# Nineteen small loads behind the third K and V transfer of a decode block on one core

## The chip, the core and the metric

The kernel runs on one core of a Trainium2 chip. The metric is the device time of one execution in microseconds, as the median of several runs. The profile is a single profiled execution on the same core, with the time of every instruction and every DMA packet.

## The reference

A transformer block for one token of each of four sequences (B = 4, D = 512), in float32. The conditioning `c` gives six modulation vectors. Attention has 32 query heads on 8 K/V heads of width 128 and sees the last 2048 positions of the cache; a gated feed-forward network of width 1792 follows.

```python
mod = (_silu(c) @ w_mod).reshape(c.shape[0], 6, 1, -1)
sa, ca, ga, sb, cb, gb = (mod[:, 0], ..., mod[:, 5])
h = _layernorm(x, axis=-1) * (1 + ca) + sa
x = x + ga * _A_ref(h, A_k_cache, A_v_cache, A_wq, A_wo)   # softmax(q k^T / sqrt(128)) v, then @ wo
h = _layernorm(x, axis=-1) * (1 + cb) + sb
x = x + gb * _B_ref(h, B_w1, B_w3, B_w2)                   # (silu(h @ w1) * (h @ w3)) @ w2
```

## The kernel before

About 101 MB are read once, and almost every tile is a slice of one SBUF ring of 192 KB for each partition, cut into three slots of 64 KB. Seven K/V groups of 8 MB each come in one transfer (`kv_in`, K in the first half of a row, V in the second); the eighth is split into `last_k_wo` and `last_v`, and the weights `wo`, `w1`, `w3` and `w2` follow. All but `wq` (ScalarE's queue) are issued by SyncE, in the order of the program text, and one transfer has 128 rows.

A helper `do` (line 57, to which the profile puts every operation) records each operation with the regions that it reads and writes. From these it derives the waits: an operation waits for the last one on another engine that touched an overlapping region, and for each DMA that did, unless it is known to be done already. Every awaited DMA has a semaphore of its own. Waits of one operation are put out in falling order of the position that the awaited operation has on its engine. Loads wait for whoever last read their slot, and this sets the order of the transfers:

- The first three loads on SP are `w_mod_a` (slot 0) and K/V group 0 (slot 2), at once, and group 1 (slot 0) when TensorE has done the modulation products.
- Group 2 goes to slot 1 when `wq` has been used. This is the "third K and V transfer", `kv[2]`.
- Group g + 3 is issued when group g has been finished, into the same slot; the first of these is `kv[3]`, behind group 0.
- Behind group 4 come the weights for the projection and the second modulation (`wom`), behind group 6 the last K and V, `wo` and `w1`; `w3` waits for the second modulation's products (`mod_columns` into `mod_b`), and `w2` comes in four pieces behind it.

The work of a group is scores on TensorE, the maximum on VectorE, the exponential on ScalarE, transposes, and the products with V. In the last part `mod_b` (128 x 512) takes the second modulation: four quarters `ga`, `sh`, `cb1` and `gb`. `x1` (128 x 128) is the residual after attention, and `h2T` (128 x 4 x 32) the transposed input of the feed-forward part, written by `transposed("h2T")`. The gate products read `h2T` and `w1`, the next ones `h2T` and `w3`, and `w2` follows.

Near the end a mark splits the program in two parts. The semaphores of the first part are cleared by GpSimd in one range when the other engines have passed the mark.

Of the kernel before, what the change touches and what calls it, by code (L numbers as in the profile page):

```python
# [9 lines left out]
P = 128  # L10
# [135 lines left out]
def block_kernel(nc, w_mod_a, wq, kv_in, wo_mod, last_k_wo, last_v, wo, w1, w3, w2, out):  # L146
# [5 lines left out]
    do = Program(nc)  # L152

    def sb(name, *shape):
        return nc.alloc_sbuf_tensor(name, (P, *shape), F32).ap()
# [12 lines left out]
    def bank():  # L168
        turn[0] += 1
        return banks[turn[0] % 2]  # L170

    def load(dst, src, cuts=(0, 1), queue="sync"):
        step = src.shape[1] // cuts[-1]
        for lo, hi in zip(cuts[:-1], cuts[1:]):
            do(queue, "dma_start", dst[:, lo * step : hi * step], src[:, lo * step : hi * step])
        return dst[:, : src.shape[1]]
# [59 lines left out]
    xc, sq, h = (sb(n, P) for n in ("xc", "sq", "h"))  # L236
# [20 lines left out]
    def transposed(name):  # L257
        hp = bank()[:, :P]
        do("tensor", "transpose", hp, h, ident)
        hT = sb(name, 4, 32)  # L260
        do("vector", "tensor_copy", hT.rearrange("p j i -> p (j i)"), hp)
        return hT

# [20 lines left out]
    do("vector", "tensor_scalar_add", mod_a[:, P:], mod_a[:, P:], 1.0)  # L284
    modulate(mod_a[:, P:], mod_a[:, :P])
    hT = transposed("hT")
    kv[1] = load(slots[0], kv_in[1])


    work = sb("work", 512)  # L290
    for half in range(2):
        qp = s_ps[half]
        for k in range(4):
            for i in range(4):
                at = ((half * 4 + i) * 4 + k) * 512
                do("tensor", "matmul", qp[32 * i : 32 * i + 32, :], hT[:, k, :], wq_t[:, at : at + 512], start=(k == 0), stop=(k == 3))
    for half in range(2):
# [4 lines left out]
        for i in range(R):  # L302
# [5 lines left out]
                src[:, :, :, None].to_broadcast([P, 4, B, NC]),  # L308
            )
    kv[2] = load(slots[1], kv_in[2])  # L310

    def project_out(g):
        for i in range(R):
            do("tensor", "matmul", a_ps[32 * i : 32 * i + B, :], oT[:, g, i, :], wo_t[g][:, i, :], start=(g == 0), stop=(g == G - 1))
# [70 lines left out]
        project_out(g)  # L385
    heads_out(G - 2)

    mod_b = sb("mod_b", 512)
    ga, sh, cb1, gb = (mod_b[:, i * P : (i + 1) * P] for i in range(4))
    mod_columns(wom[:, HALF:].rearrange("p (k j i) -> p k j i", k=4, j=4), mod_b, 4)  # L390
    do("vector", "tensor_scalar_add", cb1, cb1, 1.0)
# [8 lines left out]
    attn = bank()  # L400
    for j in range(4):
        do("tensor", "matmul", attn[32 * j : 32 * j + 32, :P], spread, work[:, j * P : (j + 1) * P], start=True, stop=True)
    x1, ag, tot2 = sb("x1", P), sq, sb("tot2", 1)
    do("vector", "tensor_mul", ag, attn[:, :P], ga)
    do("vector", "scalar_tensor_tensor", x1, ag, 1.0, x_sb, op0=ALU.mult, op1=ALU.add, accum_out=tot2)
    norm(x1, tot2)
    modulate(cb1, sh)
    h2T = transposed("h2T")

    H = P // 2  # L410
# [40 lines left out]
    for n in range(W2_CUTS[1]):  # L451
        i = n % 4
# [62 lines left out]
```

## Time and profile before

| what | value |
|---|---|
| median of two runs | 242.44 us (242.40 to 242.47) |
| the profiled execution, first to last instruction | 241.1 us |
| TensorE busy / VectorE busy / ScalarE busy | 146.8 / 55.2 / 24.0 us |
| bytes moved, mean rate | 101.38 MB, 421 GB/s |
| DMA packets in all / of SP's queue | 2889 / 2736 |
| packets under 512 bytes | 448 |
| mean granted TensorE clock | 0.865 |

The profile doesn't give what lies outside the first and the last instruction; the runs' median is 1.3 us above the span. In rows of the time line the first number is the start, the second the length, both in us; x7 after a row is the number of instructions merged in it, and a bracket gives the idle time of the engine before it and what ended it. "SPq" is SyncE's queue with its issues, whose length is that of the issuing instruction and not of the transfer. In the DMA lists the last number is the time from issue to landing.

### The profile page before, as it was taken

Reading aid. Unit: us, or ns where it says so; the run is one execution under the profiler, and the core shown is the slowest. Engines: PE = TensorE matmul, PEld = TensorE weight load, DVE = VectorE, ACT = ScalarE, POOL = GpSimd, SP = SyncE. Lnnn points to the kernel's source line nnn. Section 1 sums busy time; section 2 is a strip of 40 time slices with the busy share of each in tenths; the row PEclk is TensorE's granted clock in tenths of the full one; section 3 lists DMA queues with packets and bytes.
Section 4 is the critical chain, followed back from the end, with each engine's and each line's share of the span. In section 5 each row is a group of like instructions: output and inputs, shape, how many; then the busy total and the mean of one; then the engine's idle time right before and its main releaser. Section 6 shows DMA issues by size and latency. Waiting matters only on the chain.

```text
span 241.1 us, 2468 instructions
## 1 busy us (share of the span) xinstructions
PE 146.8 (61%) x1103; PEld 52.8 (22%) x1103; DVE 55.2 (23%) x140; ACT 24.0 (10%) x36; POOL 2.6 (1%) x11
## 2 busy tenths in 40 slices
PE   0000169756782972945767586567296919964876
PEld 0000132213222312201311222221131202422333
DVE  4000220240303124123132124130312014103120
ACT  2000000103003003001200300300300000320100
POOL 3000000000000000000000000000000000000000
PEclk9999997995977799779797589797977997996899
DMA  8999989898989898989999999999999999999993
GB/s 316 414 436 425 500 370 500 351 511 359 511 359 503 370 502 370 489 383 478 391 479 391 478 394 468 402 468 405 457 413 424 435 405 435 407 432 426 416 415 133
DMA packets 2889, 101.38 MB, mean 421 GB/s; under 512 B 448, under 2 KB 448, under 8 KB 704
## 3 DMA queue, kind: packets, MB, share of 16 engines
q1 hardware_dynamic: 2736, 92.85, 89.5%
q10 hardware_dynamic: 144, 8.39, 8.1%
q8 instruction: 8, 0.13, 0.2%
q14 instruction: 1, 0.01, 0.0%
HBM read 101.20 MB, written 0.03 MB: 420 GB/s over the span
## 4 chain that ended last, share of the span: by engine, by line
DMA 73%; PE 20%; DVE 3%; ACT 2%; issue 0%; SPq 0%
DMA ring<-kv_in 30%; DMA ring<-wo_mod 17%; DMA ring<-w 15%; DMA ring<-w_mod_a 11%; PE s_ps L57 8%; PE bank L57 7%; PE o_ps L57 4%; PE a_ps L57 2%; ACT p_sb L57 2%; DVE nm L57 2%; DVE p_sb L57 0%; DVE e L57 0%; DVE sq L57 0%; DVE xc L57 0%; DVE tot L57 0%
## 5 line engine op out<-in xcount | busy, mean ns | idle before, releaser
L57 PE MATMUL s_ps<-ring,qT 128*32 128x512 f32 x256 | 37.0, 731 | 20.2 <-DMA ring<-kv_in 14.7
L57 PE MATMUL bank<-ident,p_sb 128*128 128x128 f32 (+1 forms) x136 | 27.4, 350 | 30.8 <-ACT p_sb L57 30.7
L57 PE MATMUL o_ps<-ring,pT 128*16 128x512 f32 x256 | 37.8, 696 | 0.0
L57 PEld LDWEIGHTS bank<-ident,p_sb 128*128 128x128 f32 (+1 forms) x136 | 19.6, 177 | 51.9 <-ACT p_sb L57 31.7
L57 ACT ACTIVATE p_sb<-s_ps,nm 128x2048 f32<-128x2048 f32 (+1 forms) x11 | 16.5, 1501 | 143.2 <-DVE oT L57 105.2
L57 DVE TENSOR_REDUCE nm<-s_ps 128x1 f32<-128x2048 f32 x7 | 16.0, 2292 | 34.5 <-PE s_ps L57 34.5
L57 DVE COPY pT<-bank 128x64 f32<-128x64 f32 x32 | 7.2, 224 | 56.1 <-PE bank L57 56.1
L57 PEld LDWEIGHTS s_ps<-ring,qT 128*32 128x32 f32 x256 | 9.0, 131 | 47.5 <-issue 20.7
L57 PE MATMUL bank<-ident,xs 128*128 128x128 f32 x1 | 0.5, 473 | 27.8 <-POOL xs L57 27.8
L57 PE MATMUL s_ps<-ring,h2T 128*32 128x512 f32 (+1 forms) x64 | 9.1, 664 | 2.3 <-DMA ring<-w 2.3
L57 PE MATMUL a_ps<-ring,oT 128*4 128x512 f32 x64 | 9.1, 709 | 2.0 <-DMA ring<-wo_mod 2.0
L57 PE MATMUL s_ps<-ring,hT 128*32 128x512 f32 x64 | 8.8, 711 | 0.4 <-DVE hT L57 0.4
L57 PEld LDWEIGHTS o_ps<-ring,pT 128*16 128x16 f32 x256 | 5.4, 98 | 11.6 <-issue 9.2
L57 DVE SCALAR_TENSOR_TENSOR o_own<-o_ps,rl,own 128x512 f32<-128x512 f32 x7 | 5.3, 751 | 11.1 <-PE o_ps L57 11.1
L57 DVE TENSOR_REDUCE o_sum<-o_own 128x128 f32<-128x512 f32 x7 | 7.2, 1029 | 0.2
L57 PE MATMUL bank<-ring,sc 128*32 128x256 f32 (+1 forms) x64 | 7.2, 610 | 0.0
L57 PEld LDWEIGHTS bank<-ident,xs 128*128 128x128 f32 x1 | 0.2, 180 | 27.8 <-POOL xs L57 27.8
L57 DVE TENSOR_SCALAR e<-e 128x16 f32<-128x16 f32 x1 | 0.2, 174 | 23.8 <-ACT e L57 23.8
L57 DVE TENSOR_REDUCE mx<-s_ps 128x1 f32<-128x512 f32 x4 | 2.8, 691 | 7.6 <-PE s_ps L57 7.6
L57 DVE COPY qT<-bank 128x64 f32<-128x64 f32 x8 | 2.2, 277 | 9.8 <-PE bank L57 9.4
L57 PEld LDWEIGHTS s_ps<-ring,h2T 128*32 128x32 f32 x64 | 2.6, 129 | 7.4 <-issue 4.5
L57 PE MATMUL s_ps<-ring,hidT 128*32 128x64 f32 (+1 forms) x126 | 3.7, 262 | 0.3 <-DVE hidT L57 0.3
(93 smaller groups left out, 55.4 us busy)
## 6 DMA issues: line engine op xcount, KB each, us to landing
ring<-w SPq DMA_DIRECT2D x2, 3584.0 KB, 38.3
ring<-last_k_wo SPq DMA_DIRECT2D x1, 6144.0 KB, 30.5
ring<-last_v SPq DMA_DIRECT2D x1, 4096.0 KB, 39.9
ring<-w_mod_a SPq DMA_DIRECT2D x1, 2064.0 KB, 26.6
ring<-wo SPq DMA_DIRECT2D x1, 2048.0 KB, 43.4
ring<-w SPq DMA_DIRECT2D x1, 1792.0 KB, 40.9
ring<-w SPq DMA_DIRECT2D x1, 1024.0 KB, 42.9
ring<-w SPq DMA_DIRECT2D x1, 512.0 KB, 43.7
```

Source lines behind the costliest of these rows:

```text
L57: op = Op(engine, lambda: getattr(getattr(self.nc, engine), method)(*args, **kw), [])
```

## The change

Nineteen loads are added on SP, behind the issue of `kv[2]` and ahead of that of `kv[3]`. Fifteen of them read n rows of 4n columns (16n bytes) of `w1`, for n = 1 to 15, into the first n partitions of `mod_b`, each into columns of its own. Four read 64, 32, 8 and 112 rows of 68, 76, 80 and 72 columns into parts of `x1` and `h2T`. All of what they write is overwritten later by the copy into `mod_b`, the sum into `x1` and the copy into `h2T`. These three tiles are allocated earlier for it. The helper derives new waits: the copy into `mod_b` waits for fifteen loads, the sum for three, and the copy into `h2T` for one.

```diff
@@ transposed @@
-        hT = sb(name, 4, 32)
+        hT = h2T if name == "h2T" else sb(name, 4, 32)
@@ behind kv[2] @@
     kv[2] = load(slots[1], kv_in[2])
+    mod_b = sb("mod_b", 512)
+    for n in range(1, 16):
+        at = 2 * n * (n - 1)
+        do("sync", "dma_start", mod_b[:n, at : at + 4 * n], w1[:n, at : at + 4 * n])
+    x1, h2T = sb("x1", P), sb("h2T", 4, 32)
+    h2T_rows = h2T.rearrange("p j i -> p (j i)")
+    for dst, rows, n in ((x1[:64, :68], 64, 68), (x1[64:96, :76], 32, 76), (x1[96::4, :80], 8, 80), (h2T_rows[:112, :72], 112, 72)):
+        do("sync", "dma_start", dst, w1[:rows, 1024 : 1024 + n])
@@ ahead of the second modulation @@
-    mod_b = sb("mod_b", 512)
@@ behind the attention @@
-    x1, ag, tot2 = sb("x1", P), sq, sb("tot2", 1)
+    ag, tot2 = sq, sb("tot2", 1)
```

## The prediction

> **What bounds the kernel now.** I read the page first: the span, the row of DMA slices, the queue table and the chain that ended last.
>
> ```profile
> span 241.1 us, 2468 instructions
> ...
> DMA  8999989898989898989999999999999999999993
> ...
> q1 hardware_dynamic: 2736, 92.85, 89.5%
> ...
> DMA 73%; PE 20%; DVE 3%; ACT 2%; issue 0%; SPq 0%
> ```
>
> The DMA engines are at nine tenths or more in nearly every slice, and transfers are 73% of the chain. The 2736 packets of SP's queue are nineteen loads and stores of 144: 128 rows and sixteen more, one for each engine's signal at the end. The second view is the table by stages (length, the engines, the granted TensorE clock, the DMA share, GB/s).
>
> ```profile
> 34.00:67.00 33.00, 22.69 (x157) 7.80 (x153) 9.12 (x23) 3.25 (x4) 0.00 (x0) 0.84 0.99 429
> 67.00:86.00 19.00, 13.93 (x82) 4.93 (x82) 3.81 (x8) 2.06 (x2) 0.00 (x0) 0.73 1.01 435
> 86.00:143.00 57.00, 38.03 (x246) 13.38 (x246) 14.88 (x27) 6.17 (x6) 0.00 (x0) 0.82 1.02 439
> 143.00:183.00 40.00, 25.31 (x172) 8.52 (x164) 11.51 (x20) 4.12 (x4) 0.00 (x0) 0.87 0.97 419
> 183.00:229.00 46.00, 33.46 (x239) 11.13 (x239) 9.32 (x32) 5.32 (x14) 0.00 (x0) 0.85 1.00 428
> ```
>
> The share is 0.97 to 1.02 from 34 to 229 us, at 419 to 439 GB/s, while PE is busy for two thirds of the time at a clock below full. The kernel is a stream of loads that never runs dry; arithmetic follows each landing. So any time that the DMA engines lose before the last weights arrive is lost to the end, and any time that SP, DVE or PE lose beside a full queue is not.
>
> The third view is SP's own time line, with the consumers on PE, around the place of the edit.
>
> ```profile
> 45.73 0.33 SPq L57 DMA_DIRECT2D ring<-kv_in  x1
> ...
> 48.17 3.64 PE L57 MATMUL s_ps<-ring,qT 128*32 128x512 f32 x32 [0.57 <-DMA ring<-kv_in]
> ...
> 64.81 0.33 SPq L57 DMA_DIRECT2D ring<-kv_in  x1
> ...
> 67.28 0.64 PE L57 MATMUL s_ps<-ring,qT 128*32 128x512 f32 x4 [2.54 <-DMA ring<-kv_in]
> ...
> 86.77 0.64 PE L57 MATMUL s_ps<-ring,qT 128*32 128x512 f32 x4 [1.32 <-DMA ring<-kv_in]
> ```
>
> The third K and V transfer is issued at 45.73 and used at 86.77. The fourth is issued at 64.81, when group 0 has freed its slot, and until 86.77 it only stands behind the third. So SP idles for 64.81 - 46.06 = 18.7 us behind the edit, and a late fourth issue would start to hurt only near 86.8, 40 us later.
>
> **The change part by part.** Nothing is removed. Nineteen loads are added to SP's program behind the issue at 45.73, and the copies that later fill `mod_b`, `x1` and `h2T` get waits for them. The moved allocations issue nothing.
>
> *SP.* The price of an issue is in the rows of the weight loads.
>
> ```profile
> L57 SPq DMA_DIRECT2D ring<-w x6: 327/438/453, 181.6 to 194.7; - x6
> ...
> 194.18 0.94 SPq L57 DMA_DIRECT2D ring<-w  x2
> ```
>
> An issue takes 0.33 to 0.45 us and follows the one before it at 0.47 (two in 0.94). Nineteen take at most 8.9 us, from 46.1 to 55.0, inside the 18.7 us in which SP has nothing to issue. The shapes with fewer than sixteen rows have no row in this trace; if one took three times as long, the nineteen would end at 73 us, and the fourth transfer would still be in the queue 13 us before its turn. Cost on the path: 0. Without that cover it would be the 8.9 us.
>
> *The DMA engines.* The loads come behind the third transfer and ahead of the fourth, while the share is 1.0, so their engine time goes onto the end in full. By rows there are 1 + 2 + ... + 15 = 120, and 64 + 32 + 8 + 112 = 216: 336 rows of 16 to 320 bytes, 82 KB, which is 0.19 us at 435 GB/s. With sixteen signals each, as the old loads have, there are 304 more packets, 640 in all. The nearest packets are those of the store at the end, 128 rows of 256 bytes; its window, 239.5 to 241.1, shows it alone.
>
> ```profile
> DMA packets 144, 0.03 MB, mean 21 GB/s; under 512 B 144, under 2 KB 144, under 8 KB 144
> ...
> q1 hardware_dynamic: 144, 0.03, 9.7%
> ...
> out<-p_sb SPq DMA_DIRECT2D x1, 32.0 KB, 1.5
> ```
>
> 9.7% of sixteen engines over 1.6 us is 2.48 us for 144 packets, 17 ns each. Spread evenly, 640 packets are 40 to an engine: **0.69 us**. They will not be spread evenly, since a load of three rows can't use sixteen engines. The trace doesn't show which engines a short load uses. Bounds: if each short load runs wholly on the same engine, that one gets 120 rows, 15 signals and 17 packets of the other four loads, 152 packets or 2.6 us; from below, the engines that end last may get none of the short loads and only some 17 packets, 0.29 us. A gain is excluded here, as more bytes go through a full queue. That the engines don't end together is seen in the window 230 to 239.5 (slices of 0.24 us):
>
> ```profile
> DMA  8999996899969998998999898956454450000000
> ```
>
> The last eight slices before the end are at about half: half of the engines are done 1.9 us before the others. An engine of the early half could take all of its share unseen. I take **0.6 us**, a little under the even spread.
>
> For where the rows go the Trainium skill has a rule (DMA: Bandwidth & Descriptors, "Why a DMA increments its semaphore by 16 and not by 1"): a load issued by SP runs on the largest number of engines up to sixteen that divides both outer dimensions, on the lowest-numbered ones. By it one engine gets 29 rows and 19 signals, 0.83 us, another 13 rows and 4 signals, 0.29 us; no run here shows the numbers of the engines.
>
> *The completions.* Whether a small load holds its queue until its signal has landed is seen at the end of the weights, where two loads in a row are small for this kernel.
>
> ```profile
> ring<-w SPq DMA_DIRECT2D x1, 512.0 KB, 43.7
> ring<-w SPq DMA_DIRECT2D x1, 256.0 KB, 43.8
> ```
>
> The last was issued at 194.67, the one before it at 194.18, so they landed at 237.9 and 238.5, 0.6 us apart, and 256 KB at 435 GB/s are 0.6 us. No fixed cost per load is left in the queue: completions overlap. I take 0 and keep 0.05 us for a load as the error of reading this, 1.0 us for nineteen.
>
> *The waits on DVE.* The copy into `mod_b` gets fifteen, the sum that writes `x1` three, the copy into `h2T` one. All loads have landed by about 90 us, so what is left is the instructions, which the page doesn't count. Two DVE instructions with a wait row between them can't be seen; the closest starts in a row bound the price.
>
> ```profile
> 192.90 0.69 DVE L57 COPY mod_b<-bank 128x512 f32<-128x512 f32 x1 [3.45 <-PE bank L57]
> 193.62 0.23 DVE L57 TENSOR_SCALAR mod_b<-mod_b 128x128 f32<-128x128 f32 x1
> 200.26 0.69 DVE L57 TENSOR_REDUCE mx<-s_ps 128x1 f32<-128x512 f32 x1 [6.41 <-PE s_ps L57]
> ...
> 219.16 0.16 DVE L57 TENSOR_SCALAR ve<-bank 128x1 f32<-128x1 f32 x1 [0.93 <-ACT ln L57]
> 219.23 0.28 DVE L57 TENSOR_TENSOR xs<-xc,mod_b 128x128 f32<-128x128 f32 x1
> 219.43 0.21 DVE L57 SCALAR_TENSOR_TENSOR a<-r,ve 128x1 f32<-128x1 f32 x1
> ```
>
> Starts stand 0.07 us apart (219.16, 219.23), or 0.21 for a whole small instruction. Fifteen are 1.1 to 3.2 us behind PE's last product at 192.9; behind them on DVE stand the addition to `cb1` and then the maxima of group 7, which wait for K until 200.26 after 6.41 us of idleness. Cost 0, and 1.1 us if that cover were gone. The load of `w3`, which PE releases at the same point, is SP's and doesn't pass through this copy. The four waits near 216.8 and 220.8 cost 0.28 us, at most 0.84, on the chain from `x1` to `h2T`. Who waits for that is PE:
>
> ```profile
> 221.46 5.50 PE L57 MATMUL s_ps<-ring,h2T 128*32 128x512 f32 x32 [0.71 <-DMA ring<-w]
> ...
> 229.88 3.63 PE L57 MATMUL s_ps<-ring,h2T 128*32 128x512 f32 x32 [1.57 <-DMA ring<-w]
> ```
>
> The gate products start at 221.46 on the landing of `w1`, and the next ones at 229.88 after PE has idled 1.57 us for `w3`. A gate that is 0.28 us late is absorbed in that idle time. Cost 0; without it, 0.28.
>
> *The sum.* From the landing of `w3` at 229.88 the tail is 241.1 - 229.9 = 11.2 us of work that nothing changes, and `w3` and `w2` are later by what the DMA engines lost: 241.1 + 0.6 = 241.7 us of span. The profiled execution's span is 1.3 us below the median of the runs, 242.44, which holds what lies around it; with that unchanged, **243.0 us**.
>
> **The rivals.**
>
> *A small row costs more than a stored one.* The rows come from HBM and the price was a store's. The 256 KB load is eight rows of 2 KB on each engine in 0.6 us, 75 ns each. At that price the engine with 48 packets (29 rows, 19 signals) loses 3.6 us: 242.4 + 3.6 = **246.0**. Against it stands that those 75 ns are the bytes themselves at full rate.
>
> *SP is held at the queue.* If the queue takes only so many loads that are not done, SP stops in the middle of the nineteen, and the fourth K and V transfer with it. The fullest queue of this trace stands at 194.67.
>
> ```profile
> 167.69 0.33 SPq L57 DMA_DIRECT2D ring<-last_k_wo  x1
> 168.06 0.43 SPq L57 DMA_DIRECT2D ring<-last_v  x1
> 169.41 0.33 SPq L57 DMA_DIRECT2D ring<-wo  x1
> 181.64 13.47 SPq L57 DMA_DIRECT2D ring<-w  x6
> ...
> ring<-last_k_wo SPq DMA_DIRECT2D x1, 6144.0 KB, 30.5
> ```
>
> The last K lands at 167.69 + 30.5 = 198.2, so nine loads are outstanding: it, the last V, `wo`, `w1`, `w3` and four of `w2`, with the issue no slower. At 46 us three are outstanding, so with a limit of nine six small ones go out; one more goes when the first K and V pair lands near 48.2 and one at 67.3, and eleven are left at 86.8 when the third lands and the queue is empty. Eleven at 0.47 are 5.2 us, the fourth's issue 0.33 and its first bytes perhaps 0.8 more: 6.3 us without data, never regained. 242.4 + 6.3 + 0.6 = **249.3**, slower. It decides as soon as SP is stuck past 86.8 us. For it: the trace never shows more than nine, and here it would be 22. Against: nine loads of nine packets on each engine are 81, about what the engine with most small packets would have to hold (27 and 48).
>
> *Small loads don't overlap in their queue.* Each would then hold its engines until its signal is in. The store's 1.5 us from issue to landing less the 0.35 of the issue are 1.15; nineteen are 22 us: **264.9**, slower. The 0.6 us between the two landings speaks against it. The Trainium skill's rule of thumb (DMA: Bandwidth & Descriptors, "Rules for kernel authors" and "Anatomy of one DMA") is that a transfer below 64 KB is mostly overhead, with about 2.0 us fixed for each, measured on another issue path; nineteen would be an estimated 38 us, 280 in all. By that rule the change is clearly slower; the two landings here don't agree with it, as long as other loads stand in the queue.
>
> *A faster run*, by engines that get out of step, has no room: the stages already run at 419 to 439 GB/s with a share of 1.0. Closing the 1.9 us between the engines at the end would be all, under 2%. That the loads do nothing at all is excluded, as they are issued; if all of their cost falls on the early engines, the time is 242.4.
>
> **How the numbers follow.** The forecast, 242.2 to 243.6 around 243.0, has a chance of 0.77; the dearer row 0.06; SP held 0.10; no overlap 0.06; faster by over 2% 0.01. The range of 242.2 to 246.0 holds the first two and the 2.6 us bound, and leaves out 0.17. 2% is 4.8 us, about what a measurement of this kernel can tell from no change: slower by more are the two rivals at 249.3 and 264.9, 0.16; within 2% 0.83; faster 0.01.
>
> **What would show it.** In the changed profile SP's queue has 2736 + 640 = 3376 packets, or some hundred fewer if short loads signal on fewer engines. SP issues nineteen times between 46 and 55 us; the fourth transfer is still issued near 65 and the third used within 1 us of 86.8. The use of `w3` moves from 229.9 to 230.2 to 231, the `mod_b` copy by about 1 us behind its PE product with the first maximum of group 7 still released by PE. I am wrong if an issue of the nineteen lasts over 1 us, if the fourth transfer is issued after 86 us, or if the DMA share falls below 0.95 in the stage 86 to 143.

## The result and the profile after

The median went from 242.44 to 244.25 us, a ratio of 1.0074 with a 95% interval of 1.0045 to 1.0104: 1.8 us slower. The profiled execution has a span of 242.8 us. The page of the changed kernel, in the same parts as before:

```profile
span 242.8 us, 2498 instructions
...
DMA  8999999999999899999999999999999999999993
...
q1 hardware_dynamic: 3248, 92.93, 89.6%
...
DMA 75%; PE 19%; DVE 3%; ACT 2%; issue 0%; SPq 0%
```

It is the same stream of loads, with 512 more packets in SP's queue: 336 rows and 176 signals. With sixteen signals for each load there would have been 304. This agrees with the rule of the Trainium skill that the prediction named (DMA: Bandwidth & Descriptors, "Why a DMA increments its semaphore by 16 and not by 1"): a load of n rows, n below sixteen, runs on n engines, and 120 + 16 + 16 + 8 + 16 are 176.

SP's time line and the uses on PE around the edit, and then the last weights:

```profile
47.23 0.33 SPq L57 DMA_DIRECT2D ring<-kv_in  x1
47.61 5.28 SPq L57 DMA_DIRECT2D mod_b<-w  x15
52.93 1.93 SPq L57 DMA_DIRECT2D x<-w  x3
54.90 0.43 SPq L57 DMA_DIRECT2D h2T<-w  x1
...
66.21 0.35 SPq L57 DMA_DIRECT2D ring<-kv_in  x1
...
67.59 0.64 PE L57 MATMUL s_ps<-ring,qT 128*32 128x512 f32 x4 [1.44 <-DMA ring<-kv_in]
...
87.11 3.55 PE L57 MATMUL s_ps<-ring,qT 128*32 128x512 f32 x16 [3.09 <-DMA ring<-kv_in]
107.89 4.37 PE L57 MATMUL s_ps<-ring,qT 128*32 128x512 f32 x24 [3.24 <-DMA ring<-kv_in]
...
223.20 5.60 PE L57 MATMUL s_ps<-ring,h2T 128*32 128x512 f32 x32 [0.70 <-DMA ring<-w]
231.63 3.63 PE L57 MATMUL s_ps<-ring,h2T 128*32 128x512 f32 x32 [1.48 <-DMA ring<-w]
```

And of the kernel before, the use of the fourth transfer:

```profile
106.13 5.15 PE L57 MATMUL s_ps<-ring,qT 128*32 128x512 f32 x32 [3.50 <-DMA ring<-kv_in]
```

The steps from use to use show where the time went. Up to the third transfer the two profiles differ by 0.3 us, as they already do at 67.28 and 67.59, ahead of any small load. From the third use to the fourth it took 106.13 - 86.77 = 19.36 us before and 107.89 - 87.11 = 20.78 after: **1.42 us are lost between these two landings**, exactly where the small loads stand in the queue. Nothing is lost or regained later: the use of `w3` is 1.75 us later (229.88, 231.63), the 0.3 and the 1.42 together, and the tail from there is 11.2 us in both.

SP was no obstacle. The nineteen were issued from 47.6 to 55.3, and the fourth K and V transfer at 66.2, 21 us before its turn. The DMA share doesn't show the loss. In the stage from 86 to 143 us the prediction's table has a share of 1.02 and 439 GB/s, and the changed kernel has:

```profile
86.00:143.00 57.00, 37.95 (x246) 13.11 (x246) 13.57 (x26) 6.17 (x6) 0.00 (x0) 0.85 0.99 425
```

The share stays at 0.99, because a packet that takes longer counts as busy for all of its time; the bytes for each second are 3% fewer. A share below 0.95, one of the signs that the prediction set for being wrong, could not show this loss. So the question is why 512 packets that at 17 ns each fill sixteen engines for 0.54 us cost 1.4 to 1.8.

### The profile page after: what moved, and what is told of

It reads as the page before. It is cut to its first block, busy times and chain, and to the rows that moved or that the text cites. A ratio compares the mean times of both kernels' runs of the same rounds, so it can differ in the third digit from the quotient of the medians.

```text
span 242.8 us, 2498 instructions
## 1 busy us (share of the span) xinstructions
PE 148.8 (61%) x1103; PEld 53.0 (22%) x1103; DVE 55.3 (23%) x140; ACT 24.1 (10%) x36; POOL 2.6 (1%) x11
## 4 chain that ended last, share of the span: by engine, by line
DMA 75%; PE 19%; DVE 3%; ACT 2%; issue 0%; SPq 0%
DMA ring<-kv_in 31%; DMA ring<-wo_mod 17%; DMA ring<-w 15%; DMA ring<-w_mod_a 11%; PE bank L57 7%; PE s_ps L57 6%; PE o_ps L57 4%; PE a_ps L57 2%; ACT p_sb L57 2%; DVE nm L57 2%; DVE p_sb L57 0%; DVE e L57 0%; DVE sq L57 0%; DVE xc L57 0%; DVE tot L57 0%
## 5 line engine op out<-in xcount | busy, mean ns | idle before, releaser
L57 PE MATMUL bank<-ident,p_sb 128*128 128x128 f32 (+1 forms) x136 | 28.1, 357 | 30.8 <-ACT p_sb L57 30.7
L57 PEld LDWEIGHTS bank<-ident,p_sb 128*128 128x128 f32 (+1 forms) x136 | 20.3, 182 | 52.3 <-ACT p_sb L57 31.7
L57 PE MATMUL s_ps<-ring,hT 128*32 128x512 f32 x64 | 9.8, 780 | 0.4 <-DVE hT L57 0.4
L57 DVE COPY oT<-bank 128x16 f32<-128x16 f32 x8 | 1.3, 168 | 11.5 <-PE bank L57 11.5
```

The lines of the kernel that those rows point to most:

```text
L57: op = Op(engine, lambda: getattr(getattr(self.nc, engine), method)(*args, **kw), [])
```

## The experiments

Each kernel is the changed one with the edit shown (shortened), and was timed against the kernel before on the same chip. The microseconds behind the ratios are ratios times 242.4.

### Which of the loads

```diff
-    for n in range(1, 16): ...        # four: the fifteen out
-    for dst, rows, n in (...): ...    # fifteen: the four out
```

> Only the four larger loads (64, 32, 8 and 112 rows) stay; the fifteen short ones are taken out. Refill theory (a burst of small packets costs its own packets, some 17 ns each, and then, once, about 0.9 us in the first 64 KB rows behind it): 0.25 + 0.9 = 1.1 us over before, 243.6. Price-per-load theory (1.8 us over nineteen loads is 0.095 us for each): 0.4 us, 242.8. Uneven-rows theory (the engine with a row of every short load ends last): 0.3 us, 242.7.

> Only the fifteen short loads stay. Refill: 0.3 + 0.9 = 1.2 us, 243.6; together with the four alone clearly more than 1.8. Price per load: 1.4 us, 243.9. Uneven rows: nearly all, 1.5 us, 243.9.

The four alone: 1.0019 (1.0010 to 1.0028), 0.5 us. The fifteen alone: 1.0036 (1.0023 to 1.0048), 0.9 us. Together they would be 1.3, and the nineteen cost 1.8. The uneven-rows theory had put nearly all of it, 1.5 us, on the fifteen, and misses too. The four refute the refill theory, which I had formed from the first 64 KB rows behind the burst (in the packet records of the changed kernel half of the engines take 3.7 to 3.9 us for that row in place of 2.42): a burst of four doesn't pay it. A fixed price for each load doesn't fit either, with 0.12 us for one of the four and 0.06 for one of the fifteen; the intervals of these two overlap a little, so that by itself is not a proof.

### One small load

```diff
+    do("sync", "dma_start", mod_b[:, :64], w1[:, :64])   # in place of the nineteen
```

> One load of 128 rows of 256 bytes in place of the nineteen: eight small packets and one signal on every engine, spread evenly. Refill: 0.15 + up to 0.9 = 1.0 us, 243.4, with the first 64 KB rows behind it longer than 2.42 us. Price per load: 0.1 us, 242.5. Uneven rows: 0.15 us, 242.6.

1.0002 (0.9993 to 1.0011): no difference that can be seen. Eight small rows and one signal on each engine don't cost a start-up of the stream.

### Without the waits on VectorE

```diff
-    ... into mod_b, x1 and h2T
+    ... into mod_a, in bands of 16 partitions
+    do("gpsimd", "memset", mod_a[:, :240], 0.0)          # ahead of the last K; it waits for the nineteen
```

> The same nineteen shapes, in the same place, but into the dead tile mod_a, so that the copies into mod_b and h2T and the sum into x1 have no new waits; GpSimd, idle since 27.7 us, clears the tile behind them and waits in their place. If all of the 1.8 us is the DMA engines' (refill, price per load and uneven rows alike): 244.2. If the waits on VectorE or what hangs on them cost part: 243.8 or less.

1.0072 (1.0059 to 1.0086), 1.7 us: all of the loss is still there, so the waits are not its cause, and neither is where the rows are written. The rows of the kernel before and then of the changed one say the same:

```profile
189.17 3.64 PE L57 MATMUL bank<-ring,sc 128*32 128x512 f32 x32
...
216.50 0.29 DVE L57 TENSOR_TENSOR sq<-bank,mod_b 128x128 f32<-128x128 f32 x1 [2.81 <-PE bank L57]
216.82 0.29 DVE L57 SCALAR_TENSOR_TENSOR x<-sq,x_sb 128x128 f32<-128x128 f32 x1
```

```profile
191.03 3.64 PE L57 MATMUL bank<-ring,sc 128*32 128x512 f32 x32
...
194.76 0.69 DVE L57 COPY mod_b<-bank 128x512 f32<-128x512 f32 x1 [3.45 <-PE bank L57]
...
218.33 0.29 DVE L57 TENSOR_TENSOR sq<-bank,mod_b 128x128 f32<-128x128 f32 x1 [2.82 <-PE bank L57]
218.66 0.29 DVE L57 SCALAR_TENSOR_TENSOR x<-sq,x_sb 128x128 f32<-128x128 f32 x1
```

PE's last product ends at 194.67, and the copy with the fifteen waits starts 0.09 us later, as before (192.81 and 192.90). The sum with three more waits starts 0.33 us behind its predecessor (0.32 before).

### Completions or packets

By now the theory was that an engine is slow at *finishing* loads in close order. Each load that uses an engine ends on it with a signal. The fifteen short loads allow a closer look, because each has its own row size: the packets of one engine can be followed through the trace by the sizes 16, 32, ... 240. By this reconstruction of mine from the packet records of that run, the engine that finished fifteen loads lost 1.9 us up to the end of its next 64 KB row, those with ten to twelve 1.4, the one with eight 0.9, with seven 0.4, and with six or fewer 0.3 or less. Two kernels, each with other loads in place of the nineteen, separate completions from small packets and from uneven loads:

```diff
+    for n in range(15):                                   # even15
+        do("sync", "dma_start", mod_b[:16, 16*n : 16*n+16], w1[:16, 16*n : 16*n+16])
+    do("sync", "dma_start", <128 rows x 4 pieces of 16>, <the same of w1>)   # pieces
```

> Fifteen loads of 16 rows of 64 bytes in place of the nineteen: every engine gets one row and one completion of each, fifteen rows in all, as the most loaded engine of the fifteen short loads had. Completion theory (behind more than some six loads in a row on one engine, each further one leaves about 0.12 us, seen in the first 64 KB row behind the burst): 1.7 to 1.9 us on all sixteen engines, 244.2, more than the fifteen short loads (0.9). Uneven-rows theory (only engines that stand apart from the others cost): 0.35 us, 242.8. Price for each load, whatever it is (0.06 by the fifteen): 0.9 us, 243.3.

> One load of 128 rows of four pieces of 64 bytes: 32 small packets on every engine, as many as the most loaded engine had, and a single completion. Completion theory: the packets alone, 32 at 12 to 17 ns, 0.4 to 0.5 us, 242.9, and no first 64 KB row of over 3 us. Small-packet theory (what is slow is many small packets in a row): 1.4 us or more, 243.8.

The uses of the third and fourth transfers on PE, first with the fifteen even loads and then with the pieces:

```profile
86.96 3.89 PE L57 MATMUL s_ps<-ring,qT 128*32 128x512 f32 x20 [2.00 <-DMA ring<-kv_in]
108.32 3.92 PE L57 MATMUL s_ps<-ring,qT 128*32 128x512 f32 x20 [3.34 <-DMA ring<-kv_in]
```

```profile
87.12 3.37 PE L57 MATMUL s_ps<-ring,qT 128*32 128x512 f32 x16 [2.27 <-DMA ring<-kv_in]
106.59 3.64 PE L57 MATMUL s_ps<-ring,qT 128*32 128x512 f32 x32 [1.92 <-DMA ring<-kv_in]
```

Fifteen rows of 64 bytes with fifteen completions on each engine: 1.0092 (1.0078 to 1.0105), 2.2 us, and 21.36 us from use to use, 2.0 more than before. Thirty-two such rows with a single completion: 1.0014 (1.0005 to 1.0022), 0.3 us, and 19.47. The first has 480 packets more than the kernel before, signals included (3216 in SP's queue), the second 528 (3264). So with more than twice the small rows, about as many packets and one fifteenth of the completions the loss is a seventh. Small packets are cheap; loads that end one right behind the other are not. The uneven-rows theory, which gave the even loads 0.35 us, is out.

### How many

```diff
-    for n in range(15):
+    for n in range(5):      # even5; range(30) for even30
```

> Five loads of 16 rows of 64 bytes, one row and one completion on every engine for each. Serial-completion theory (an engine finishes a completion every 0.14 us, as 2.1 us for fifteen say, with some slack ahead of it): 0.2 to 0.7 us, 242.6 to 243.1. Price by the queue's burst, whatever its length: 2.1 us, 244.5.

> Thirty such loads. Serial completions at 0.14 us each: 4.2 us, 246.6, and first 64 KB rows of 6 us or more. A stall that comes once, when some limit is first reached: 2.1 us and 15 more pairs of packets at 13 ns, 2.3, 244.7.

Five: 1.0011 (1.0002 to 1.0020), 0.3 us. Thirty: 1.0222 (1.0208 to 1.0236), 5.4 us. The uses with five, and with thirty:

```profile
86.73 3.54 PE L57 MATMUL s_ps<-ring,qT 128*32 128x512 f32 x16 [3.01 <-DMA ring<-kv_in]
106.14 3.64 PE L57 MATMUL s_ps<-ring,qT 128*32 128x512 f32 x32 [1.86 <-DMA ring<-kv_in]
```

```profile
86.82 3.64 PE L57 MATMUL s_ps<-ring,qT 128*32 128x512 f32 x32 [1.91 <-DMA ring<-kv_in]
110.83 1.93 PE L57 MATMUL s_ps<-ring,qT 128*32 128x512 f32 x8 [8.31 <-DMA ring<-kv_in]
```

From use to use it is 19.41 and 24.01 us: 0.05 and 4.65 over before. From fifteen to thirty loads each adds (5.4 - 2.2) / 15 = **0.21 us** by the medians and (24.01 - 21.36) / 15 = **0.18 us** by the uses. The difference is 0.7 us that the kernel with thirty loses later, before the use of `w3` (at 235.24, 5.36 us behind the kernel before); that part was not followed. A line through fifteen and thirty meets zero at about four loads, and the five lie near it. So the stall is not one that comes once: the first few completions are covered by what the engine has under way, and every further one is paid. My 0.14 us for each, without a free beginning, was too low.

The trace shows the pace itself. It keeps the time at which each signal reached its semaphore, and a load has landed when its last signal has. These are the issues of the thirty loads (shortest, median and longest in ns, then the first and last start) and their time to landing:

```profile
L57 SPq DMA_DIRECT2D mod_b<-w x30: 416/420/2381, 46.0 to 62.0; - x30
...
DMA to landing us min/median/max: 30.2/35.8/41.0
```

The first load lands at 46.0 + 41.0 = 87.0 and the last at 62.0 + 30.2 = 92.2. The 29 steps between them take 5.2 us, **0.18 us** for each. Yet by the packet records all of their 960 small packets, signals included, are through by 86.7. With fifteen even loads the landings go from 87.09 to 89.72, 0.19 us apart, and with five from 86.86 to 87.52, 0.17 apart. So the rows pass quickly, and the signals of a burst arrive one after the other, at nearly the same pace whether there are five or thirty. In the changed kernel the signals of the engine that all nineteen loads use arrive from 85.35 to 88.67, again 0.18 us apart. The 64 KB row behind a burst begins meanwhile. With fifteen and with thirty loads it ends 1.2 us behind the last signal of its engine, on all sixteen engines (ends and signals paired in order of time), where such a row takes 2.42 us otherwise. So about a microsecond of signals, some five of them, is hidden beside that row, and the rest is lost. This is an estimate from these numbers, and it agrees with the line above.

```diff
+        do("sync", "dma_start", <16 rows of 256 elements of mod_b>, <the same of w1>)   # even15_1k
```

> Fifteen loads of 16 rows of 1024 bytes in place of 64, so that an engine moves 15 KB, 0.57 us at its full rate, in the burst. If completions are finished one after the other at 0.14 us and the rows' own time runs beside that: 2.1 to 2.3 us, 244.6, as with 64 bytes. If a load's price comes on top of its bytes: 2.1 + 0.45 = 2.6 us, 245.0.

1.0109 (1.0095 to 1.0122), 2.6 us, where the rows of 64 bytes had cost 2.2. The medians say that the bytes come on top of the completions, but the two intervals overlap a little, so that is not settled. These loads are written to other partitions and read from other parts of the rows of `w1` than the ones of 64 bytes, so the loss doesn't hang on one place in memory.

### Spread out, on the other queue, and at the end

```diff
+    some(0) ... some(4)            # spread: every fifth of the nineteen behind each of five K and V transfers
-    do("sync", "dma_start", ...)   # act: the nineteen issued by ScalarE instead
+    do("scalar", "dma_start", ...)
```

> The nineteen loads into the dead tile, four behind each of five K and V transfers (three behind the last) and not all behind the third; GpSimd waits for them. Completion theory: no more than four in a row, so only packets, 0.5 us, 242.9. Price for each load, wherever it stands: 1.8 us, 244.2.

> The nineteen loads into the dead tile, issued by ScalarE on its own queue in front of group 0's exponential, so that they run beside the 64 KB rows of SP's queue. Completion theory: each small packet takes its turn with a 64 KB row, so completions are 2.4 us apart and cost nothing: 0.3 to 0.6 us, 242.9. Price for each load: 1.8 us, 244.2. ScalarE is held for about 8 us near 47, which group 0 pays and the queue covers.

Spread: 1.0026 (1.0016 to 1.0037), 0.6 us. On ScalarE's queue: 1.0027 (1.0017 to 1.0038), 0.7 us. Both have the same nineteen loads with the same rows, and about a third of the loss. What is left is what the packets alone were expected to take. On ScalarE's queue the signals of an engine arrive some 2.4 us apart, one behind each 64 KB row of SP's queue. Neither kernel is faster than the one without the loads.

```diff
+    w2_t = load(...); nineteen("sync", mod_a); do("gpsimd", "memset", ...)   # end: behind w2
```

> The nineteen loads into the dead tile, issued behind the last piece of w2, where no weight is queued behind them; GpSimd waits for them. If the cost is only what stands behind the burst in the queue: 0 to 0.3 us, 242.5. If it comes from the program itself (more instructions, semaphores, the start of the kernel): 0.4 us or more of the 1.8 stay.

1.0046 (1.0034 to 1.0059), 1.1 us: by its size this would speak for the second theory, that the cost lies in the program, but the rows show another reason. The third and fourth transfers are used 19.37 us apart, so the stream lost nothing there; the new time is elsewhere.

```profile
86.81 3.64 PE L57 MATMUL s_ps<-ring,qT 128*32 128x512 f32 x32 [1.79 <-DMA ring<-kv_in]
106.18 6.05 PE L57 MATMUL s_ps<-ring,qT 128*32 128x512 f32 x28 [3.55 <-DMA ring<-kv_in]
...
239.78 0.36 SPq L57 DMA_DIRECT2D out<-p_sb  x1
241.33 0.30 POOL L57 MEMSET mod_a<- 128x240 f32 x1 [213.33 <-DMA mod_a<-w]
```

The output is issued only 0.2 us later than before (239.56). But GpSimd waits until 241.3 for the small loads. The packets of the nineteen are through by 238.7, and their last signal arrives at 241.28, 2.6 us later: the slow completions again, now at the very end. The span is 0.5 us longer than before, and the other 0.6 of the 1.1 us lie outside it; GpSimd, which clears the semaphores, is late for that, but no row shows it. So this kernel has a new end of its own, and it doesn't tell whether a few tenths of the 1.8 come from the program around the loads.

## Why the prediction was right or wrong

The time lies on the side that the point forecast had; the point, 243.0, is 1.25 us short. It is above 242.2 to 243.6, the part that had a chance of 0.77. It is inside the wider range up to 246.0 only because that was stretched for a dearer row and for one engine with all of the short loads, and neither of these is what happened. That the range holds the time is luck as far as the mechanism goes. By steps:

- **What bounds the kernel**: right. The loss made between two landings at 87 and 108 us arrives unchanged at the end.
- **SP**: right. 7.7 us of issues for 8.9 estimated, all under the idle time.
- **The packets**: right in size. By the runs with one completion or few in a row (pieces, spread) the packets are worth 0.3 to 0.6 us. (The prediction gave the least loaded engine four signals. The four larger loads alone left 56 in SP's queue, 3008 packets less 2736 and 216 rows, so the one of 8 rows signals on eight engines, and such an engine has three.)
- **The completions**: this is the step that failed. I took 0 with a bound of 1.0 us, because the last two pieces of `w2` landed 0.6 us apart, which their bytes explain. Those two leave 0.6 us between their completions on an engine, and small loads in a row leave some 15 ns between the packets of their signals. The row showed that one completion at a time is hidden; it could not show a dozen. In its place the runs showed 0.18 to 0.21 us for each beyond the first four or five on an engine. There are 3 to 19 completions on an engine, eleven on average. An estimate from that average is 6.5 times 0.21, some 1.4 us, against the missing 1.2; engine by engine it wasn't worked out. The prediction had a real price for a completion only in its rival at 264.9, and nothing between that and a reading error of 0.05 us.
- **The slack of the early engines**: right in kind. With fifteen short loads the busiest engine lost 1.9 us and the kernel 0.9; with fifteen even loads the fourteen engines that could be followed lost 1.4 to 2.4 and the kernel 2.2. In the kernel before, fourteen engines signal the end of the third transfer between 84.91 and 85.39 and the other two at 86.59 and 86.73, so most engines have over 1 us to spare. That a load on few engines falls in part on engines that would have been early fits these numbers; no run moved the loads to the two late engines.
- **The waits on DVE**: priced at 1.1 and 0.28 us behind cover; the copy and the sum show no delay at all.
- **What a measurement can tell**: wrong. The prediction took 2%, 4.8 us, as about the least; the 0.5 us of the four loads alone stand clear of no change.
- **No overlap between small loads** (264.9): wrong as priced, yet the nearest in kind: the signals of an engine do come one after the other. One costs 0.18 to 0.21 us, under a fifth of the 1.15 us taken there, and the rows don't wait for it.
- **SP held at the queue** (249.3): it did not happen here, with 21 loads outstanding and no issue above 0.72 us. But the effect exists. In the kernel with thirty loads the last two take 1.9 and 2.4 us to issue (the row is shown above), and in the one with the nineteen behind `w2` all are slow:

```profile
L57 SPq DMA_DIRECT2D mod_a<-w x19: 940/2067/3821, 195.6 to 228.0; - x19
```

  The kernel with the nineteen behind `w2` was held at its tenth outstanding load, the one with thirty took 28 small ones on top of two large, so the limit doesn't count loads, as the rival supposed. In packets for each engine both were near seventy (nine loads of nine packets, the oldest nearly done; or 28 pairs, nine packets of the third transfer and what was left of the second). That is an estimate from two runs; the edge itself wasn't tried. The changed kernel's most loaded engine, 48 small packets beside some fourteen, stood just below it. One issue at the start of the runs with fifteen and with thirty even loads took 1.1 to 1.5 us as well, with few loads outstanding, and this isn't explained.

What stays open is what an engine waits for in the 0.18 us before each signal. The runs show that the loss goes with the number of loads that end on an engine in close order, that the rows are through long before the signals arrive, and that the loss appears for the most part in the first large row behind them (3.7 to 3.9 us in place of 2.42 on half of the engines with the nineteen). With nineteen or thirty loads some of the last small packets take longer too, 0.1 to 0.4 us each. No kernel had loads without a completion of their own.

## What to carry to other kernels

A queue that is always full has no free place for small loads: count, for each engine, how many loads end on it in a row. Up to four or five were all but hidden here (0.3 us with five); each one more cost about 0.2 us of the whole stream, with rows of 64 bytes and little more with 1024, so many small loads should be put together into one, or be dealt out between large ones, or go on another queue. A row in which two loads follow one another at half a microsecond says nothing of a dozen within a fifth of a microsecond.

## What the runs showed of the hardware

- Thirty-two rows of 64 bytes on each engine in one load cost 0.3 us; fifteen such rows in fifteen loads 2.2 us, and thirty in thirty loads 5.4 us.
- Signals of small loads reach their semaphores 0.17 to 0.19 us apart, with five, fifteen or thirty loads, while the packets of two signals on an engine are some 15 ns apart.
- Behind fifteen and thirty such loads the next 64 KB row on an engine, 2.42 us otherwise, ends 1.2 us after the last of these signals.
- The same nineteen loads cost 1.8 us in one burst behind a 64 KB row, 0.6 us in five groups of four, and 0.7 us beside the large rows on the other queue.
- An issue on SP takes 0.23 to 0.7 us in the changed kernel and up to 3.8 us behind nine loads of 128 rows that are not done.
